# Retuning a hand-written planner: paired ramps, full P.V rounds and packs of four in a two-layer attention and gMLP kernel

## The chip, the cores and the metric

The kernel runs on one core of one Trainium2 chip. The metric is the device time in microseconds (us) of one execution; lower is better. Five executions of the kernel before took 1650.32, 1652.5, 1651.31, 1657.53 and 1656.46 us, with a median of 1652.5 us. A profile was taken of one execution, and all views below are of that one.

The engines are named as in the profile: PE (TensorE, matmuls; PEld is its weight loads), DVE (VectorE), ACT (ScalarE), POOL (GpSimd) and SP (SyncE, which issues DMAs).

## The reference

Two layers, each an attention block and a gMLP block, on one sequence of 2048 positions with width 512. The attention has 32 query heads of 16 channels that share one key and one value head.

```python
def _A_ref(x, wq, wk, wv, wo):
    q = (x @ wq).reshape(B, S, H, Dh).transpose(0, 2, 1, 3)   # H=32, Dh=16
    k = x @ wk
    v = x @ wv
    scores = einsum('bhqd,bkd->bhqk', q, k) * Dh ** (-0.5)
    o = einsum('bhqk,bkd->bhqd', softmax(scores), v)
    return o.transpose(0, 2, 1, 3).reshape(B, S, H * Dh) @ wo

def _B_ref(x, w_in, w_sp, b_sp, w_out):                        # F=1792, Fh=896
    z = gelu(x @ w_in)
    z1, z2 = z[..., :Fh], layernorm(z[..., Fh:])
    g = einsum('ts,bsf->btf', w_sp, z2) + b_sp[None, :, None]
    return (z1 * g) @ w_out

x = A_x
x = x + _A_ref(layernorm(x), ...)
x = x + _B_ref(layernorm(x), ...)
x = x + _A_ref(layernorm(x), ...)
x = x + _B_ref(layernorm(x), ...)
```

## The kernel before

The program of each engine is written out by a planner in the kernel's Python. `Sched` holds a modelled clock, a list of ready tasks for each engine and a model cost for each task; `Kernel.run` moves the modelled clock from event to event and lets each free engine take one step (`step_act`, `step_dve`, `step_pool`, `step_pe`, `step_sp`). The order in which tasks are taken becomes the fixed instruction order of that engine, with semaphore waits put in where a task needs another engine's result. So the constants at the top of `Kernel` (about L380 to L418) do not touch any instruction's work. They decide which tasks are formed, how they are grouped, and in which order each engine runs them.

**Attention.** Per layer there are 2048 score blocks. One block is 128 keys by 512 (query, head) columns, for one of four groups of PE rows j. A *pack* is one to four blocks, one per j, which PE computes side by side (`issue_pack`, matmul at L1227); each block fills one bank of PSUM, of which there are eight. `pack_ready` (L1153) says whether a pack may be issued and how large it is: up to `score_cap` banks may hold scores, 6 when the layer's first 128 blocks are out (`A.full`) and 4 before that. A pack of fewer than four is allowed only if ACT's modelled backlog is at most `ACT_LOW`.

A block's exponential is made in one of two ways:

- by ACT, as an `Exp` activation of one bank or of two adjacent banks at once (`pick_exp` L1367, `do_exp`, instruction at L1402). The result is one slot of `Pb`, a buffer of 32 slots in SBUF. Two banks at once need two adjacent banks and two adjacent free slots. With `ACT_ONE` = 3, when the queue holds one pack alone and at least three of its blocks, ACT takes a single first.
- by DVE and POOL (`dve_block` L1294), which approximate the exponential with integer arithmetic as a weighted sum of three piecewise linear *ramps*. DVE reads the scores and writes the first ramp (L1316, called an A task here). The two other ramps are made from the first one, by POOL or by DVE (`ramp_fn`, L1335, called S tasks), one slot each. `commit_ramp` (L1337) joins two S tasks of the same kind into one instruction of 1024 columns when their sources lie in adjacent slots and two adjacent slots are free.

How many blocks of a pack go the second way is a running credit in `issue_pack`: each block adds `SHARE`, `SHARE_HI` or, before a layer is full, `RAMP_SHARE`. One is held back when DVE's backlog is over `DVE_HIGH`.

**P.V.** PE multiplies each finished slot with the values, in four groups of columns j side by side (`do_pv`, L1457). Up to four matmuls, one per j, form a *round*. A block of ACT brings one matmul, a block of DVE three. `pv_depth` (L1519) says how many rounds a visit does: at most `PV_MAX`, and only if the rounds are filled to `PV_EFF`; when PE comes from another kind of work, a visit also needs `PV_LEAST` matmuls. When fewer than 8 slots are free it goes ahead anyway.

**The rest.** Queries are taken in eight chunks. When a chunk is done, its output is normalised, projected and added, and the gMLP of its rows begins (`mlp_in`: gelu on ACT in a batch, with a load of ACT's table before and after; `spatial`: the product with `w_sp`, L1083). This lies beside the attention of later chunks. After the last chunk only the last pass (`last_pass`, L1114 and L1116), the output product (L1138) and the residual (L1142) are left; each tile of 128 rows then feeds the layer norm, keys and queries of the next layer, so that layer's first blocks begin between the two. `step_pe` orders PE: gelu batches first, then a pack, then P.V, then other matmuls that fit before the next pack is due or that have waited longer than `MISC_T`.

`step_dve` takes tasks that only DVE can do first. It takes an S task only if POOL is idle and POOL's backlog is over `POOL_MAX`. `step_pool` takes whatever is ready by priority.

Of the kernel before, what the change touches and what calls it, by code (L numbers as in the profile page):

```python
# [10 lines left out]
ALU = mybir.AluOpType  # L11
# [8 lines left out]
S = 2048  # L20
# [21 lines left out]
def c_ps(cols):  # L42
    return 70 + 1.042 * cols, 130
# [49 lines left out]
class Sched:  # L93
# [69 lines left out]
    def commit(self, task, eng=None):  # L163
        t = self.t
        eng = eng or task.eng
        task.eng = eng
        if task.alts is not None:
            task.cost, task.fn = task.alts[eng]
        task.start = t
        if task.hook is not None:  # L170
            task.hook(task)
        cost = task.cost() if callable(task.cost) else task.cost
        occ, lat = cost
        if eng == "pe" and task.mode != self.pe_mode:
            occ += 100
            self.pe_mode = task.mode
        port = eng == "dve" and task.tag in PORT
        if port:
            occ += max(0.0, self.free["pool"] - t)
        end = t + occ  # L180
        self.free[eng] = end
        if port:
            self.free["pool"] = max(self.free["pool"], end)
        self.busy[eng] += occ
        task.done = end + lat
        waits = self._waits(eng, task)
        if eng == "sp":
            k = min(range(self.NDMA), key=lambda i: (self.dma_last[i].done if self.dma_last[i] else -1.0))
            prev = self.dma_last[k]
            if prev is not None:  # L190
                waits += self._wait_on(eng, prev)
            self.dma_n[k] += 16
            task.key, task.val = ("dma", k), self.dma_n[k]
            self.dma_last[k] = task
        else:
            self.cnt[eng] += 1
            task.key, task.val = eng, self.cnt[eng]
        s = dict(self.know[eng])
        if s.get(task.key, 0) < task.val:
            s[task.key] = task.val  # L200
        self.snap[(task.key, task.val)] = s
        self.prog[eng].append((waits, task.fn, task.key, task))
        self.log.append((eng, t, end, task.tag))
        if eng == "pe":
            self.pe_log.append((t, end))
        self.left -= 1
        for s_ in task.succ:
            s_.nopen -= 1
            if s_.nopen == 0:
                self._arm(s_)  # L210
        self.event(end)
        self.event(task.done)
        while self.after:
            self.after.pop(0)()
        return task
# [164 lines left out]
class Kernel:  # L380
# [1 line left out]
    SCORE_CAP = 6  # L382
    WSP_FROM = 25000
    NPS = 32
    PV_FREE = 6
    KT_ACT = 16
    CREDIT = 2
    CAP_LINE = 8000
    RAMP_SHARE = 0.3
    Q_LATE = 2  # L390
    PORT_WAIT = 0
    NWS = 8
# [1 line left out]
    GP_PRIO = 0.95  # L394
    SP_PRIO = 3.5
    NROT = (2, 2)
    SHARE = 0.3
    SHARE_HI = 0.32
    PE_LINE = 5000
    WARM = 0.6  # L400
    FILL_MIN = 2
    ACT_LOW = 1200
    POOL_MAX = 1400
    DVE_MAX = 1500
    DVE_HIGH = 2500
    PV_MIN = 3
    PV_MAX = 3
    PV_EFF = 0.7
    PV_LEAST = 4
    SLACK = 300  # L410
    SLACK_HI = 500
    MISC_T = 2000
    MISC_T2 = 1500
    MISC_T3 = 1000
    PE_LINE2 = 8000
    ACT_ONE = 3
    ACT_MAX = 2

    def __init__(self, nc, es, ins, out):
# [733 lines left out]
    def pack_ready(self):  # L1153
        if self.ai >= len(self.attns) or (self.batch is not None and not self.batch.pe_done):
            return None
        A = self.attns[self.ai]
        av = self.banks.avail()
        room = min(4, len(av), self.score_cap() - self.score_held)
        if room < self.FILL_MIN or room < 4 and self.act_backlog() > self.ACT_LOW:
            return None  # L1160
        blks = []
        deps = []
        for (u, kt, j) in A.blocks[A.nxt:A.nxt + room]:
            ds = A.kdep[kt] + [A.qdep[t] for t in range(u.q0 // P, (u.q0 + u.nq) // P)]
            if any(d.start is None or d.done > self.s.t for d in ds):
                break
            deps += ds
            blks.append((u, kt, j))
        if not blks or len(blks) < room and len(blks) < 4 and A.nxt + len(blks) < len(A.blocks) and self.act_backlog() > self.ACT_LOW:
            return None  # L1170
        return A, blks, deps, av

# [17 lines left out]
    def issue_pack(self, A, blks, deps, bs):  # L1190
        s = self.s
        k = len(blks)

        x = self.RAMP_SHARE if not A.full else self.SHARE if self.pe_line() > self.PE_LINE else self.SHARE_HI
        self.credit = min(self.credit + k * x, self.CREDIT) if x else 0.0
        late = sum(1 for u, kt, j in blks if kt >= self.KT_ACT)
        nd = min(2, k - 1, k - late, int(self.credit))
# [6 lines left out]
        aj = [i for i in range(k) if i not in dj]  # L1204

        best = None
        for act in itertools.combinations(sorted(bs, key=lambda b: b.i), len(aj)):
            runs = sum(1 for x, y in zip(act, act[1:]) if y.i != x.i + 1)
            key = (runs, sum(b.i for b in act))
            if best is None or key < best[0]:  # L1210
                best = (key, act)
        act = list(best[1])
# [38 lines left out]
        av = sum(1 for b in self.pslots.items if not b.held and b.free <= self.s.t)  # L1251
        return av - k >= sum(v for m, v in self.need.items() if m < n)

    def slot_runs(self):
        free = {b.i: b for b in self.pslots.avail()}
        runs = []
        for i in sorted(free):
            if i - 1 in free:
                runs[-1].append(free[i])
            else:  # L1260
                runs.append([free[i]])
        return sorted(runs, key=lambda r: (len(r), r[0].i))
# [5 lines left out]
    def first_slot(self):  # L1268

        runs = self.slot_runs()  # L1270
        free = {b.i: b for r in runs for b in r}
        for i in self.open_slots:
            for k in (i - 1, i + 1):
                if k in free:
                    self.open_slots.remove(i)
                    return free[k], True
        for r in runs:
            if len(r) > 1:
                return r[0], False
        return runs[0][0], False  # L1280
# [13 lines left out]
    def dve_block(self, pk, u, kt, j, bank, n):  # L1294
# [7 lines left out]
            sl[v] = b  # L1302
            self.need[n] -= 1

        def h0(task):
            b, paired = self.first_slot()
            slot(0, b, task, T)
            if not paired:
                self.open_slots.append(b.i)

            def go():
                self.free_bank(bank, task)
                u.av[j].append((task.done, task, sl[0], 1, kt))
            self.after.append(go)
        lo0 = float(TERMS[0][0])
        a = self.dve(c_ps(512), lambda e: e.tensor_scalar(self.Pi[:, sl[0].i, :], self.ps32[:, bank.i, :], EBIAS + lo0, lo0, op0=ALU.add,  # L1316
                                                          op1=ALU.max), [pk], 1.0, gate=lambda: self.slot_ok(n, 1), hook=h0, tag="A")
        for v in range(1, T):

            def hv(task, b=None, v=v):  # L1320
# [9 lines left out]
            k = self.either({"pool": (c_pool(512), fn), "dve": (c_4x(512), fn)}, [a], 3, gate=lambda: self.slot_ok(n, 1), hook=hv, tag="S")  # L1330
            k.ramp = (v, sl, n)

    def ramp_fn(self, v, src, dst, k):
        lo = float(TERMS[v][0])
        return lambda e: e.tensor_scalar(self.Pi[:, dst():dst() + k, :], self.Pi[:, src():src() + k, :], lo, 1.0, op0=ALU.add, op1=ALU.mult)  # L1335

    def commit_ramp(self, k, eng):  # L1337

        s = self.s
        v, sl, n = k.ramp  # L1340
        for it in s.arm[eng]:
            p = it[2]
            if p.ramp is None or p.start is not None or p.ready > s.t or p.ramp[0] != v or abs(p.ramp[1][0].i - sl[0].i) != 1:
                continue
            m = max(n, p.ramp[2])
            if not self.slot_ok(m, 2):
                continue
            run = self.pair_slots()
            if run is None:
                continue  # L1350
            two = sorted((k, p), key=lambda x: x.ramp[1][0].i)
            i, o = two[0].ramp[1][0].i, run[0].i
            f = Task(eng, (c_pool if eng == "pool" else c_4x)(1024), self.ramp_fn(v, lambda: i, lambda: o, 2), k.deps + p.deps, tag="S")

            def hook(task):
                for x, b in zip(two, run):
# [2 lines left out]
            s.left += 1  # L1359
            s.commit(f)  # L1360
            for x in two:
                x.start, x.done, x.key, x.val = f.start, f.done, f.key, f.val
                s.left -= 1
            return
        s.commit(k, eng)

    def pick_exp(self):  # L1367
        q = [x for x in self.act_q if x[0].done <= self.s.t][:self.ACT_MAX]
        av = sorted((b for b in self.pslots.items if not b.held and b.free <= self.s.t), key=lambda b: b.i)
        free = {b.i: b for b in av}  # L1370

        most = len(q)
# [146 lines left out]
    def pv_depth(self, pv, room):  # L1519
# [4 lines left out]
        hurry = self.pv_hurry(pv)  # L1524
        if hurry:
            most = max(most, 1)
        for r in range(most, 0, -1):
            n = sum(min(len(x), r) for x in ls)
            if hurry or n >= 4 * r * self.PV_EFF and (sw == 0 or n >= self.PV_LEAST):
                return r  # L1530
# [116 lines left out]

    def step_dve(self):
        s = self.s
        k = s.pick("dve", lambda k: k.alts is None or "pool" not in k.alts)  # L1650

        if k is None and s.free["pool"] <= s.t + self.PORT_WAIT and self.backlog("pool") > self.POOL_MAX:
            k = s.pick("dve")
# [5 lines left out]
            s.commit(k, "dve")  # L1659
        return True  # L1660

    def step_pool(self):
        k = self.s.pick("pool")
        if k is None:
            return False
        if k.ramp is not None:
# [127 lines left out]
```

## Time and profile before

| what | value |
|---|---|
| the profiled execution | 1650.3 us, span of its instructions 1648.6 us |
| median of five executions | 1652.5 us |
| score matmuls (L1227) | 4096 |
| `Exp` on two banks / on one (ACT, L1402) | 948 / 946 |
| first ramps (DVE, L1316) | 1254 |
| later ramps on POOL, two slots / one | 421 / 976 |
| later ramps on DVE, two slots / one | 236 / 218 |
| P.V matmuls (L1457) | 6604 |
| ACT busy, 50 to 762 us (layer 0) | 688 of 712 us |
| ACT busy, 762 to 890 us (between the layers) | 57 of 128 us |
| ACT busy, 890 to 1580 us (layer 1) | 664 of 690 us |

The counts give the shares: 948 x 2 + 946 = 2842 blocks on ACT and 1254 on DVE are 4096 together, and 2842 + 3 x 1254 = 6604 P.V matmuls. "Busy" of an engine is the time in which at least one of its instructions runs. A `128x512` instruction works on one slot or bank, a `128x1024` one on two.

### The profile page before, as it was taken

Reading aid. Unit: us, or ns where it says so; the run is one execution under the profiler, and the core shown is the slowest. Engines: PE = TensorE matmul, PEld = TensorE weight load, DVE = VectorE, ACT = ScalarE, POOL = GpSimd, SP = SyncE. Lnnn points to the kernel's source line nnn. Section 1 sums busy time; section 2 is a strip of 40 time slices with the busy share of each in tenths; the row PEclk is TensorE's granted clock in tenths of the full one; section 3 lists DMA queues with packets and bytes.
Section 4 is the critical chain, followed back from the end, with each engine's and each line's share of the span. In section 5 each row is a group of like instructions: output and inputs, shape, how many; then the busy total and the mean of one; then the engine's idle time right before and its main releaser. Section 6 shows DMA issues by size and latency. Waiting matters only on the chain.

```text
span 1648.6 us, 36831 instructions
## 1 busy us (share of the span) xinstructions
PE 1555.6 (94%) x14016; PEld 528.8 (32%) x14016; DVE 1404.9 (85%) x2556; ACT 1445.9 (88%) x2067; POOL 1183.0 (72%) x1616
## 2 busy tenths in 40 slices
PE   6999999999999999999998998999999999899999
PEld 3333233222322223233433332322223222322345
DVE  7799878898788887988977998798897998788877
ACT  5999999999999998995447999999998999899940
POOL 6888868778778867774456877777876778778730
PEclk8999999999999989999999999999999999999999
DMA  8000000100001110101110000011000101001021
GB/s 212 11 8 5 8 8 17 33 17 15 14 15 26 21 21 10 31 17 36 23 31 17 9 4 8 7 30 33 14 15 14 27 14 27 14 14 27 18 42 53
DMA packets 123996, 39.76 MB, mean 24 GB/s; under 512 B 116272, under 2 KB 123312, under 8 KB 123824
## 3 DMA queue, kind: packets, MB, share of 16 engines
q1 hardware_dynamic: 123824, 37.41, 10.5%
q8 instruction: 115, 1.88, 0.5%
q14 instruction: 57, 0.47, 0.1%
HBM read 6.98 MB, written 2.10 MB: 6 GB/s over the span
## 4 chain that ended last, share of the span: by engine, by line
PE 52%; ACT 31%; DVE 10%; issue 2%; POOL 2%; DMA 2%; DVEq 0%; ACTq 0%; POOLq 0%
ACT Pb L1402 30%; PE ps_all L1457 16%; PE ps_all L1227 14%; PE ps_all L1083 8%; DVE Pb L1316 4%; PE ps_all L976 3%; PE ps_all L1022 3%; PE ps_all L1138 3%; DVE Pb L1335 2%; POOL Pb L1335 2%; PE ps_all L761 1%; PE ps_all L920 1%; DMA onT<-o_norm 1%; PE ps_all L834 1%; PE ps_all L1114 1%
## 5 line engine op out<-in xcount | busy, mean ns | idle before, releaser
L1402 ACT ACTIVATE Pb<-ps_all 128x512 bf16<-128x512 f32 (+1 forms) x1894 | 1349.9, 885 | 75.4 <-PE ps_all L1227 65.2
L1335 POOL TENSOR_SCALAR Pb<-Pb 128x512 int16<-128x512 int16 (+1 forms) x1397 | 1065.1, 762 | 301.5 <-DVE Pb L1316 130.6
L1316 DVE TENSOR_SCALAR Pb<-ps_all 128x512 int16<-128x512 f32 x1254 | 830.1, 684 | 134.5 <-PE ps_all L1227 119.2
L1457 PE MATMUL ps_all<-Pb,V 128*32 128x512 bf16 x6604 | 625.6, 389 | 16.1 <-ACT Pb L1402 5.9
L1227 PE MATMUL ps_all<-Q,kT 32*128 32x512 bf16 x4096 | 570.8, 386 | 48.5 <-ACT Pb L1402 27.9
L1227 PEld LDWEIGHTS ps_all<-Q,kT 32*128 32x128 bf16 x4096 | 147.0, 91 | 540.1 <-ACT Pb L1402 307.1
L1457 PEld LDWEIGHTS ps_all<-Pb,V 128*32 128x32 bf16 x6604 | 150.3, 94 | 305.4 <-issue 123.0
L1335 DVE TENSOR_SCALAR Pb<-Pb 128x1024 int16<-128x1024 int16 (+1 forms) x454 | 205.1, 474 | 16.8 <-PE ps_all L1457 13.4
L1083 PE MATMUL ps_all<-wstr,z 128*128 128x512 bf16 x840 | 213.8, 381 | 2.7 <-POOL z L1004 0.4
L1091 DVE TENSOR_TENSOR gp<-ps_all,gp 128x512 f16<-128x512 f32 x168 | 112.9, 686 | 26.0 <-PE ps_all L1083 24.0
L1083 PEld LDWEIGHTS ps_all<-wstr,z 128*128 128x128 bf16 x840 | 67.4, 97 | 101.3 <-issue 15.5
L1138 PE MATMUL ps_all<-w_out,z 128*128 128x512 bf16 x224 | 55.9, 380 | 1.7 <-DVE z L1124 1.3
L976 PE MATMUL ps_all<-w_in,xnT 128*128 128x448 bf16 x256 | 52.4, 361 | 2.6 <-ACT Pb L1402 1.2
L1036 ACT ACTIVATE z<-ps_all 128x512 bf16<-128x512 f32 (+1 forms) x60 | 31.3, 566 | 23.6 <-PE ps_all L1022 23.6
L1022 PE MATMUL ps_all<-xnT,w_in 128*128 128x512 bf16 (+2 forms) x280 | 51.5, 337 | 0.0
L593 POOL TENSOR_SCALAR ln_rs<-ln_mv 128x1 f32<-128x1 f32 (+2 forms) x48 | 11.2, 237 | 54.7 <-DVE ln_mv L603 53.3
L818 DVE CAST oT<-ps_all 128x512 bf16<-128x512 f32 x64 | 43.7, 683 | 4.5 <-PE ps_all L1457 4.1
L989 DVE BATCH_NORM_STATS2 st<-z 128x6 f32<-128x448 bf16 x64 | 36.3, 606 | 12.4 <-ACT z L981 12.0
L1091 DVE TENSOR_TENSOR gp<-ps_all,bspc 128x512 f16<-128x512 f32 x56 | 38.5, 687 | 9.1 <-PE ps_all L1083 8.1
L602 DVE BATCH_NORM_STATS2 ln_st<-X 128x6 f32<-128x512 bf16 x64 | 43.1, 679 | 2.7 <-DMA X<-in_A_x_dram 2.5
L593 POOL TENSOR_SCALAR rs<-mv 128x4 f32<-128x4 f32 (+2 forms) x10 | 2.3, 234 | 56.0 <-DVE mv L991 56.0
L920 PE MATMUL ps_all<-wo,onT 128*128 128x512 bf16 x128 | 38.4, 387 | 3.4 <-DMA onT<-o_norm 3.4
(67 smaller groups left out, 706.4 us busy)
## 6 DMA issues: line engine op xcount, KB each, us to landing
out_dram<-X SPq DMA_DIRECT2D x16, 128.0 KB, 1.7
w_in<-in_B_w_in_dram SPq DMA_DIRECT2D x1, 1792.0 KB, 12.0
X<-in_A_x_dram SPq DMA_DIRECT2D x3, 512.0 KB, 6.5
bspc<-in_B_b_sp_dram SPq DMA_DIRECT2D x8, 128.0 KB, 3.5
w_out<-in_B_w_out_dram SPq DMA_DIRECT2D x1, 896.0 KB, 12.7
wstr<-in_B_w_sp_dram SPq DMA_TRANSPOSE x40, 3.9
X<-in_A_x_dram SPq DMA_DIRECT2D x2, 256.0 KB, 3.0
wq<-in_A_wq_dram SPq DMA_DIRECT2D x1, 512.0 KB, 4.6
```

The costliest lines, as they stand in the source:

```text
L818: ev = Task("dve", c_ps(512), lambda e, u=u, k=k: e.tensor_copy(self.oT[:, k, :], self.ps32[:, u.bank.i, :]), [self.oT_use[k]], 0.2, tag=" ...
L920: ins = e.matmul(self.ps32[:, b, :], self.onT[:, c, t % 4, :], self.wo[:, c, :], start=(c == 0), stop=(c == 3))
L976: ins = e.matmul(self.ps32[:, b, 0:448], self.xnT2[:, buf, kd, o:o + P], self.w_in[:, kd, FH + h * 448:FH + (h + 1) * 448], start=(kd == 0 ...
L1022: ins = e.matmul(self.ps32[:, b, i * nq:(i + 1) * nq], self.w_in[:, kd, f * P:(f + 1) * P], self.xnT2[:, buf, kd, 0:nq], start=(kd == 0), ...
L1083: ins = e.matmul(self.ps32[:, b, :], self.z2[:, (s0 + i) % 8, f * P:(f + 1) * P], self.wstr[:, sl[i // 4][1] + i % 4, :], start=(i == 0), ...
L1091: return Task("dve", c_ps(512), lambda e: e.tensor_tensor(self.gp[:, tc, f, :], self.ps32[:, bank(), :], src, ALU.add), dps, 1.05, tag="gp")
L1138: ins = e.matmul(self.ps32[:, b, :], self.z1[:, tc, f, o:o + P], self.w_out[:, f, :], start=(f == 0), stop=(f == NF - 1))
L1227: ins = e.matmul(self.ps32[:, jb[i].i, :], self.kT[32 * j:32 * j + 32, u.half, kt * P:(kt + 1) * P], q, tile_position=(32 * j, 0), start=T ...
L1316: a = self.dve(c_ps(512), lambda e: e.tensor_scalar(self.Pi[:, sl[0].i, :], self.ps32[:, bank.i, :], EBIAS + lo0, lo0, op0=ALU.add, op1=AL ...
L1335: return lambda e: e.tensor_scalar(self.Pi[:, dst():dst() + k, :], self.Pi[:, src():src() + k, :], lo, 1.0, op0=ALU.add, op1=ALU.mult)
L1402: return e.activation(self.Pb[:, s0:s0 + n, :], self.ps32[:, b0:b0 + n, :], ACTF.Exp, scale=ESCALE)
L1457: ins = e.matmul(self.ps32[32 * j:32 * j + 32, u.bank.i, :], self.V[:, var, kt, :], self.Pb[:, sl.i, :], tile_position=(0, 32 * j), start= ...
```

## The change

The change edits constants and decision rules of the planner. No kind of instruction is new; what is computed stays the same, apart from which blocks are approximated by ramps.

- Shares: `SHARE`/`SHARE_HI` 0.30/0.32 become 0.32/0.34. `RAMP_SHARE` becomes 0.32 for layer 0 and 0 for layer 1 (`RAMP_SHARE1`).
- Before layer 1 is full, only packs of four are issued (`FILL_R`, `ACT_LOW_R`).
- `ACT_LOW` 1200 becomes 1400, `DVE_HIGH` 2500 becomes 1800, `ACT_ONE` 3 becomes 9.
- P.V: at most two rounds a visit, filled to 0.97, and six matmuls at least after other work.
- Slots next to a lone first ramp are kept free of exponentials while at least 8 others are free (`kept`), and banks are chosen so that DVE's blocks come to lie side by side (`A_ADJ`).
- DVE looks first for a pair of later ramps when POOL is idle and has over 4000 ns of backlog; POOL starts nothing when it has such a backlog and DVE will be free within 200 ns.
- Other matmuls count as late earlier (`MISC_T` 2000/1500/1000 become 1000/1000/500), and the planner's cost of a change of PE mode is 110 in place of 100.

`A_TWO`, `PAIRS` and `PV_R` are 0, so what they guard does not run.

```diff
@@ Kernel
-    PV_FREE = 6
+    PV_FREE = 8
+    A_TWO = 0
+    KEEP = 8
+    PAIRS = 0
+    POOL_TOP = 4000
+    HOLD = 200
+    A_ADJ = 1
-    RAMP_SHARE = 0.3
+    RAMP_SHARE = 0.32
-    SHARE = 0.3
-    SHARE_HI = 0.32
+    SHARE = 0.32
+    SHARE_HI = 0.34
+    FILL_R = 4
+    ACT_LOW_R = 0
+    PV_R = 0
+    RAMP_SHARE1 = 0.0
-    ACT_LOW = 1200
+    ACT_LOW = 1400
-    DVE_HIGH = 2500
+    DVE_HIGH = 1800
-    PV_MAX = 3
-    PV_EFF = 0.7
-    PV_LEAST = 4
+    PV_MAX = 2
+    PV_EFF = 0.97
+    PV_LEAST = 6
-    ACT_ONE = 3
+    ACT_ONE = 9
@@ pack_ready
-        if room < self.FILL_MIN or room < 4 and self.act_backlog() > self.ACT_LOW:
+        low = self.ACT_LOW if A.full or A.layer == 0 else self.ACT_LOW_R
+        if room < (self.FILL_MIN if A.full or A.layer == 0 else self.FILL_R) or room < 4 and self.act_backlog() > low:
             return None
@@ issue_pack
-        x = self.RAMP_SHARE if not A.full else self.SHARE if self.pe_line() > self.PE_LINE else self.SHARE_HI
+        x = (self.RAMP_SHARE, self.RAMP_SHARE1)[A.layer] if not A.full else self.SHARE if self.pe_line() > self.PE_LINE else self.SHARE_HI
...
+        pend = [it[2].ramp[3] for it in s.arm["dve"] if it[2].tag == "A" and it[2].start is None]
         for act in itertools.combinations(sorted(bs, key=lambda b: b.i), len(aj)):
             runs = sum(1 for x, y in zip(act, act[1:]) if y.i != x.i + 1)
-            key = (runs, sum(b.i for b in act))
+            rest = sorted([b.i for b in bs if b not in act][:nd] + pend)
+            key = (runs - self.A_ADJ * sum(1 for x, y in zip(rest, rest[1:]) if y == x + 1), sum(b.i for b in act))
@@ slots: kept() is new; slot_runs() and pick_exp() leave its slots out
+    def kept(self):
+        if not self.KEEP:
+            return set()
+        free = {b.i for b in self.pslots.avail()}
+        r = set()
+        for i in self.open_slots:
+            for k in (i + 1, i - 1):
+                if k in free and k not in r:
+                    r.add(k)
+                    break
+        return r if len(free) - len(r) >= self.KEEP else set()
@@ step_dve
-        k = s.pick("dve", lambda k: k.alts is None or "pool" not in k.alts)
+        k = None
+        if s.free["pool"] <= s.t + self.PORT_WAIT and self.backlog("pool") > self.POOL_TOP:
+            k = self.ramp_pair("dve")
+        if k is None:
+            k = s.pick("dve", lambda k: k.alts is None or "pool" not in k.alts)
@@ ramp_pair() is new: a ready later ramp whose neighbour is ready too
+    def ramp_pair(self, eng):
+        s = self.s
+        rs = [it[2] for it in s.arm[eng] if it[2].ramp is not None and it[2].ramp[0] and it[2].start is None and it[2].ready <= s.t]
+        at = {(k.ramp[0], self.place(k)): k for k in rs}
+        if len(rs) < 2 or self.pair_slots() is None:
+            return None
+        for k in rs:
+            p = at.get((k.ramp[0], self.place(k) + 1))
+            if p is not None and self.slot_ok(max(k.ramp[2], p.ramp[2]), 2):
+                s.arm[eng] = [i for i in s.arm[eng] if i[2] is not k]
+                return k
+        return None
@@ step_pool
+        if s.t < s.free["dve"] <= s.t + self.HOLD and self.backlog("pool") > self.POOL_TOP:
+            return False
```

## The prediction, written before the result

> **What bounds the kernel now.** I read the page first (busy time and the 40 slices), then busy time by stage, then ACT's waits in one stage, then the groups kept apart by shape, and last a stretch of PE's order.
>
> Page, busy time, and ACT's row of the slices:
>
> ```profile
> PE 1555.6 (94%) x14016; PEld 528.8 (32%) x14016; DVE 1404.9 (85%) x2556; ACT 1445.9 (88%) x2067; POOL 1183.0 (72%) x1616
> ...
> ACT  5999999999999998995447999999998999899940
> ```
>
> The averages put PE first. The slices say otherwise: ACT is full but for the start, four slices in the middle and the end. Busy time of the stages (us; PE, PEld, DVE, ACT, POOL):
>
> ```profile
> 50.00:762.00 712.00, 681.80 (x6148) 213.90 (x6147) 612.78 (x1094) 688.06 (x986) 552.02 (x729) 0.99 0.08 16
> 762.00:890.00 128.00, 117.85 (x1048) 53.84 (x1045) 107.68 (x221) 57.03 (x84) 58.45 (x104) 0.99 0.16 33
> 890.00:1580.00 690.00, 655.47 (x5959) 207.82 (x5957) 594.01 (x1051) 664.45 (x950) 536.95 (x704) 1.00 0.08 17
> ```
>
> Waits of ACT from 50 to 762 us (us in total, times, longest):
>
> ```profile
> ACT z L1036 <- PE ps_all L1022: 10.9, 16, 1.1
> ACT Pb L1402 <- PE ps_all L1227: 5.9, 17, 1.0
> ACT z L981 <- PE ps_all L976: 3.0, 8, 0.8
> ACT Pb L1402 <- PE ps_all L1457: 2.1, 5, 1.0
> ```
>
> In layer 0 ACT idles 24 of 712 us, and 14 of these are gelu batches. Its exponentials wait 9 us. So ACT's work sets the pace of the two long stretches. Between them ACT has half its time free, and PE (118 of 128) and DVE (108) take turns on the chain.
>
> Groups by shape (busy us, mean ns of one, idle before):
>
> ```profile
> L1402 ACT ACTIVATE Pb<-ps_all 128x1024 bf16<-128x1024 f32 x948 | 952.9, 1098 | 47.6 <-PE ps_all L1227 42.8 <-PE ps_all L1457 2.6 <-DVE Pb L1335 0.6
> L1402 ACT ACTIVATE Pb<-ps_all 128x512 bf16<-128x512 f32 x946 | 546.3, 671 | 27.8 <-PE ps_all L1227 22.4 <-PE ps_all L1457 3.5 <-DVE Pb L1335 0.5
> L1335 POOL TENSOR_SCALAR Pb<-Pb 128x512 int16<-128x512 int16 x976 | 616.0, 631 | 224.4 <-DVE Pb L1316 108.2 <-PE ps_all L1457 44.5 <-PE ps_all L1227 8.4
> L1335 DVE TENSOR_SCALAR Pb<-Pb 128x1024 int16<-128x1024 int16 x236 | 131.7, 573 | 7.8 <-PE ps_all L1457 5.0 <-POOL Pb L1335 0.4
> ```
>
> The means are latencies, and neighbours overlap. The distance from one start to the next is the price; its medians in the trace are 904 ns for a double `Exp`, 478 for a single, 608 for a first ramp, 700 and 1127 for a single and a double ramp on POOL. PE's order, 163 to 166 us (start, us):
>
> ```profile
> 163.36 0.39 PE L1227 MATMUL ps_all<-Q,kT 32*128 32x512 bf16 x3
> 163.69 0.40 PE L1457 MATMUL ps_all<-Pb,V 128*32 128x512 bf16 x4
> 164.02 0.39 PE L1227 MATMUL ps_all<-Q,kT 32*128 32x512 bf16 x2
> 164.34 0.62 PE L761 MATMUL ps_all<-z,wq 128*128 128x128 bf16 x8
> ```
>
> A pack and a round of P.V each cost about 0.32 us however many of the four lanes are filled.
>
> **What the Trainium skill says.** "TensorEngine Tiling (Array Packing)", Key Properties: a change of tiling mode drains PE. The trace agrees: a lone round goes from start to start in 332 ns, two rounds in 547, so 215 for a round and about 115 for the change. "SBUF — State Buffer", Who interferes with whom: a VectorE instruction in a two-port mode and a GpSimd instruction exclude each other for a whole instruction, and the later one waits. The trace agrees: of DVE's 236 double ramps, 139 began while POOL was running and took 681 ns on average; the other 97 took 419. "Perfetto Trace Analysis", Identifying the Most-Contended Engine: matmul busy time is no measure of PE's headroom. Here PE is 96% busy in a stretch where ACT hardly waits for it.
>
> **The change, part by part.**
>
> *Shares.* Of 4096 blocks, 256 come before a layer is full and 3840 after. Before: about 0.30 x 256 = 77 of the 1254 first ramps fall in the 256, so 1177 in the 3840. The constants rise by 0.02: 77 more blocks go to DVE in ACT's full stretches. At about 460 ns a block on ACT that is at most 36 us. `DVE_HIGH` at 1800 holds some back, and held credit is lost above 2; as far as it cuts deeper than now it could cost half as much (+18). DVE must find 77 x 0.6 = 46 us, of 99 idle in layer 0 and 96 in layer 1; the 154 further ramps cost about 0.5 us each on POOL, 77 of some 310 idle. They fit, but DVE and POOL are needed in time, not on average. I take 60%: **-21 us** (-36 to +18).
>
> *Pairs on ACT.* Without the single-first rule a pack of three gives a double first, and the third may join the next pack. Two singles cost 956, a double 904: 52 ns a pair. There are 886 singles in the two stretches (454 and 432), so all of them would give 23 us. Packs stay small (I count 1530 packs, 2.7 blocks on average), and one block is often alone after DVE's share. I take a quarter: 111 pairs, **-6 us** (-23 to 0). Slots kept for ramps narrow the choice of two adjacent ones; that is why not more.
>
> *Ramps on DVE and POOL.* A double on DVE that finds POOL idle saves 262 ns over one that waits; over 139 it is 36 us of DVE. POOL's hold costs at most 0.2 us each time. No chain runs through it while ACT is full; this is what makes room for the 46 us above. Counted at **0**; if DVE were the bound it would be worth up to those 36 us.
>
> *P.V in full rounds.* I count 1260 visits with 5.2 matmuls on average, about 1900 rounds where 6604/4 = 1651 are needed. After: 6604 + 2 x 39 = 6682 matmuls (39 more ramp blocks net: 77 more when full, 38 fewer before), 835 visits of two rounds at 0.548 us, 458 us against 581 now. PE gains some 120 us, but ACT hides it: ACT waits 9 us for PE in layer 0. The price is in slots: finished slots wait until every lane has two. POOL waited 65 us on P.V for slots already, ACT 6. I take **+4** (0 to +80).
>
> *Between the layers.* The 128 first blocks of layer 1 lose 0.3 x 128 = 38 first ramps. That frees DVE of 38 x 0.6 = 23 us and PE of 76 P.V matmuls. From 800 to 890 us the trace has 132 blocks in 55 packs and 208 P.V matmuls in 44 visits; after, 33 packs (22 x 0.32 = 7 us off PE) and about 130 matmuls in 17 visits of 0.55 (some 9 us against 20). The last pass, keys and layer norm gain from both: of 90 us, perhaps 20. Against it: with a cap of four banks, a pack of four waits until all four banks are free. PE 0.32, two doubles 1.8, and about 0.2 until PE sees it make 2.3 us a pack, 74 us for 32, near the 90 there are. The blocks wait for keys as well, tile by tile. I take **-8** (-20 to +15).
>
> *The other constants.* Lateness of other matmuls and the cost of 110 only reorder PE, which has room: 0. `ACT_LOW` at 1400 makes small packs come sooner; PE pays 0.32 each out of the 120 us: 0. The start and the 69 us of PE after the last `Exp` stay.
>
> Sum: -21 - 6 + 4 - 8 = -31. From the profiled execution's 1650.3 this gives 1619.3; the median of the runs stands 2.2 higher, so I say **1621**.
>
> **The rivals.**
> - *Everything lands (12%).* ACT's work falls by 36 and 23 us, its waits for PE in both stretches (18) go with PE's new room, and 20 come between the layers: -97, of which contention leaves about 75: **1577**. For it: PE gains 120 us. Against: 52 ns a pair needs neighbours in banks and slots at once.
> - *DVE and POOL become the bound (20%).* ACT gives up work that they do not finish in time; first ramps already have DVE waiting on packs (56 us in layer 0), and POOL on first ramps (56). Then only pairs and the middle remain, about -10: **1642**, ranging over no change.
> - *Slower: slots run out (20%).* P.V waits for full rounds, `Pb` fills, and ACT stands before a P.V visit. At 835 visits, each 10 ns that ACT waits costs 8 us; from 37 ns a visit the 31 us are gone. At 60 ns: +50 - 31 = **1671**. For it: 32 slots, some kept free. Against: ACT waited only 6 us on P.V, and below 8 free slots P.V goes anyway.
>
> **How the numbers follow.** The forecast has 48%. Its own range is 1605 to 1638. Of the second rival about a fifth lies within 0.3% (5 us, what can be told apart here) and a tenth is slower. Faster: 48 + 12 + 14 = 74%; same 4%; slower 2 + 20 = 22%. The range for 8 in 10 leaves out the far half of the first rival and of the third: 1590 to 1668.
>
> **What would show it.** Right: about 1295 first ramps, none for layer 1 before it is full; ACT full with some 2800 blocks; P.V visits near 8; double ramps on DVE near 420 ns; the middle below 128 us. Wrong: ACT idle in the long stretches behind P.V or packs, fewer first ramps than 1254, more singles, or a longer middle.

## The result, and the profile after

The changed kernel takes 1649.8 us (median of 29 executions, 1640.5 to 1655.5). The kernel before takes 1653.6 us in 50 executions shared with it. The ratio is 0.9968 with a 95% interval of 0.9958 to 0.9977: 3.8 us faster at the medians, where 31 were forecast. The profiled execution took 1651.3 us with a span of 1649.6, so it lies 1.5 us above its median. The profiled one before lay 3.2 below the median of the 50, which is why the two spans (1648.6 and 1649.6) do not show the gain.

The page of the changed kernel, busy time, the slices of DVE, ACT and the clock granted to PE, and the chain that ended last:

```profile
PE 1516.2 (92%) x14216; PEld 506.9 (31%) x14216; DVE 1452.7 (88%) x2624; ACT 1442.9 (87%) x2052; POOL 1111.2 (67%) x1378
...
DVE  7899989999799898998865999799897999799887
ACT  5999989999899898996479989899998999899950
...
PEclk7899899999999899999999999999899999999999
...
PE 45%; DVE 28%; ACT 23%; issue 3%; DMA 1%; POOL 0%; SPq 0%; DVEq 0%; POOLq 0%
```

The same line of the kernel before:

```profile
PE 52%; ACT 31%; DVE 10%; issue 2%; POOL 2%; DMA 2%; DVEq 0%; ACTq 0%; POOLq 0%
```

DVE's part of the chain has gone from 10% to 28%, and ACT's from 31% to 23%. ACT makes fewer exponentials now (2802 blocks, 2842 before). ACT's row has eights where it had nines, and the clock has more dents.

By stage (busy us of PE, PEld, DVE, ACT and POOL), to be read beside the same rows in the prediction:

```profile
50.00:762.00 712.00, 663.42 (x6222) 204.54 (x6223) 645.79 (x1138) 671.68 (x977) 535.09 (x637) 0.98 0.08 17
762.00:890.00 128.00, 113.84 (x1162) 55.04 (x1166) 88.90 (x192) 84.93 (x109) 26.23 (x54) 1.00 0.15 29
890.00:1580.00 690.00, 636.96 (x5984) 194.73 (x5976) 626.70 (x1100) 648.20 (x917) 517.11 (x612) 0.98 0.10 16
```

In the first stretch ACT now idles 40 us (24 before), and DVE is busy 646 us (613 before). In the same stretch the score matmuls of PE wait longer for banks that DVE's first ramps still hold (us in total, times, longest; the kernel before, then the changed one):

```profile
PE ps_all L1227 <- DVE Pb L1316: 3.8, 9, 0.8
PE ps_all L1240 <- DVE Pb L1362: 15.0, 40, 1.0
```

The stages can be timed by the score matmuls, counted in order of their starts:

| stage (us) | before | after | difference |
|---|---|---|---|
| start to block 128 of layer 0 | 67.2 | 69.7 | +2.5 |
| block 128 to the last block of layer 0 | 693.8 | 700.1 | +6.3 |
| last block of layer 0 to block 128 of layer 1 | 124.5 | 112.3 | -12.2 |
| block 128 of layer 1 to the end | 763.1 | 767.5 | +4.4 |

So the middle brought what was forecast and more, and the two long stretches, which were to bring most of the 31 us, did not get faster. Together they are 10.7 us longer here; some 5 us of that is only the distance of these two executions from their medians. The groups of the changed kernel by shape (busy us, mean ns of one, idle before) show where:

```profile
L1367 DVE TENSOR_SCALAR Pb<-Pb 128x1024 int16<-128x1024 int16 x371 | 220.8, 615 | 7.4 <-PE ps_all L1503 6.0
L1367 DVE TENSOR_SCALAR Pb<-Pb 128x512 int16<-128x512 int16 x111 | 41.1, 376 | 3.3 <-PE ps_all L1503 3.3
L1367 POOL TENSOR_SCALAR Pb<-Pb 128x1024 int16<-128x1024 int16 x576 | 617.8, 1073 | 153.8 <-DVE Pb L1362 79.1 <-PE ps_all L1503 31.1 <-DVE Pb L1367 8.9
L1448 ACT ACTIVATE Pb<-ps_all 128x1024 bf16<-128x1024 f32 x923 | 921.3, 1067 | 53.8 <-PE ps_all L1240 41.5 <-PE ps_all L1503 5.4 <-DVE Pb L1367 1.2
```

DVE has 371 double ramps (236 before), but one takes 615 ns (573 before). Of the 371, 204 began while POOL was running (with at least 30 ns of its instruction left) and took 776 ns on average; the other 167 took 417. These are called collisions below. In 144 of the 204 the double ended 270 to 290 ns after the POOL instruction that it had met: it waited for POOL to end. A double takes 418 ns and a single 284 with POOL idle. What DVE's ramps take beyond that is called their *excess* here: 83 us in all, against 55 before.

One such place, DVE and then POOL from 700 us on in the timeline (start us, length us):

```profile
700.69 1.88 DVE L1362 TENSOR_SCALAR Pb<-ps_all 128x512 int16<-128x512 f32 x3
702.49 1.18 DVE L1367 TENSOR_SCALAR Pb<-Pb 128x1024 int16<-128x1024 int16 x1
703.59 0.67 DVE L1101 TENSOR_TENSOR gp<-ps_all,gp 128x512 f16<-128x512 f32 x1
```

```profile
700.09 4.05 POOL L1367 TENSOR_SCALAR Pb<-Pb 128x1024 int16<-128x1024 int16 x4 [0.51 <-PE ps_all L1503]
```

POOL runs four ramps end to end, and the double on DVE takes 1.18 us in the middle of them. In the plan POOL stands aside here: the planner keeps it free until the double is done. But the plan only orders each engine's own instructions; waits are written for results that a task needs, and POOL's next ramp needs nothing of DVE's double. Its inputs are there, so it starts.

### The profile page after: what moved, and what is told of

Its sections match the earlier page's. It is cut to its first block, busy times and chain, and to the rows that moved or that the text cites. A ratio compares the mean times of both kernels' runs of the same rounds, so it can differ in the third digit from the quotient of the medians.

```text
span 1649.6 us, 36882 instructions
## 1 busy us (share of the span) xinstructions
PE 1516.2 (92%) x14216; PEld 506.9 (31%) x14216; DVE 1452.7 (88%) x2624; ACT 1442.9 (87%) x2052; POOL 1111.2 (67%) x1378
## 4 chain that ended last, share of the span: by engine, by line
PE 45%; DVE 28%; ACT 23%; issue 3%; DMA 1%; POOL 0%; SPq 0%; DVEq 0%; POOLq 0%
ACT Pb L1448 22%; DVE Pb L1362 14%; PE ps_all L1503 12%; PE ps_all L1240 12%; DVE Pb L1367 8%; PE ps_all L1093 7%; PE ps_all L986 3%; PE ps_all L1032 3%; PE ps_all L1148 3%; DVE gp L1101 2%; PE ps_all L771 1%; DVE ln_st L612 1%; DVE oT L828 1%; DVE X L934 1%; PE ps_all L930 1%
## 5 line engine op out<-in xcount | busy, mean ns | idle before, releaser
L1367 POOL TENSOR_SCALAR Pb<-Pb 128x512 int16<-128x512 int16 (+1 forms) x1159 | 990.5, 855 | 340.1 <-DVE Pb L1362 194.5
L1362 DVE TENSOR_SCALAR Pb<-ps_all 128x512 int16<-128x512 f32 x1294 | 843.2, 680 | 90.7 <-PE ps_all L1240 81.2
L1240 PE MATMUL ps_all<-Q,kT 32*128 32x512 bf16 x4096 | 587.4, 392 | 89.9 <-ACT Pb L1448 33.3
L1503 PE MATMUL ps_all<-Pb,V 128*32 128x512 bf16 x6684 | 533.4, 394 | 15.4 <-DVE Pb L1367 4.4
L1240 PEld LDWEIGHTS ps_all<-Q,kT 32*128 32x128 bf16 x4096 | 152.7, 91 | 621.6 <-ACT Pb L1448 364.2
L1367 DVE TENSOR_SCALAR Pb<-Pb 128x1024 int16<-128x1024 int16 (+1 forms) x482 | 258.8, 560 | 10.8 <-PE ps_all L1503 9.4
L1503 PEld LDWEIGHTS ps_all<-Pb,V 128*32 128x32 bf16 x6684 | 120.0, 95 | 239.6 <-issue 119.0
L771 PE MATMUL ps_all<-z,wq 128*128 128x128 bf16 x512 | 41.1, 225 | 2.0 <-DVE Pb L1362 1.7
```

The costliest lines, as they stand in the source:

```text
L1240: ins = e.matmul(self.ps32[:, jb[i].i, :], self.kT[32 * j:32 * j + 32, u.half, kt * P:(kt + 1) * P], q, tile_position=(32 * j, 0), start=T ...
L1503: ins = e.matmul(self.ps32[32 * j:32 * j + 32, u.bank.i, :], self.V[:, var, kt, :], self.Pb[:, sl.i, :], tile_position=(0, 32 * j), start= ...
```

## The experiments

Sixteen kernels ran. Times are medians, and each ratio is to the kernel before in runs shared with it. For those that keep the plan of the changed kernel, every engine has the same instructions in the same order, but for what the edit names. The expectations say *port* for what a double of DVE and an instruction of POOL exclude each other from, as the prediction describes it. *Half clock* is time in which the profile shows PE at half its clock.

**Does POOL's missing wait cost the gain, or does the clock?** Theory 1: the collision just shown. Theory 2: PE runs at half clock more often, 51 us of the profiled execution, 17 before (counted in stretches that begin between 60 and 1600 us).

*e1_hold*: each POOL instruction also waits for the two-port instruction of DVE that the plan put before it.

```diff
         port = eng == "dve" and task.tag in PORT
+        if eng == "pool" and self.last_port is not None:
+            task.extra.append(self.last_port)
+        if port:
+            self.last_port = task
```

> The changed kernel with the same plan, and one thing more in the emitted programs: each GpSimd instruction waits for the VectorE ramp, layer-norm or z2 instruction in a two-port mode that the plan put before it. Theory 1 (the room that GpSimd leaves exists in the plan only; nothing in the program makes GpSimd wait, so it starts its next ramp and VectorE's double ramp stands behind it): double ramps on VectorE that begin while GpSimd runs fall from 204 of 371 to under 80, their mean from 615 to under 500 ns, and the time falls by 8 to 15 us below the 1649.8 of the changed kernel. Theory 2 (TensorE's clock drops to half more often, 51 us of the stretches in place of 17): the time stays within 3 us. Rival to both: GpSimd waits for VectorE too long and its ramps come late: 3 to 15 us slower.

Measured 1606.3 us, ratio 0.9708 (0.9683 to 0.9733). Its groups and its chain:

```profile
L1372 DVE TENSOR_SCALAR Pb<-Pb 128x1024 int16<-128x1024 int16 x371 | 154.1, 435 | 6.9 <-PE ps_all L1508 5.0
L1372 DVE TENSOR_SCALAR Pb<-Pb 128x512 int16<-128x512 int16 x111 | 35.4, 325 | 4.3 <-PE ps_all L1508 4.2
```

```profile
ACT 47%; PE 41%; DVE 7%; issue 3%; DMA 2%; POOL 1%; DVEq 0%; SPq 0%; ACTq 0%
```

The same place as above, with the wait (DVE, then POOL):

```profile
680.11 1.87 DVE L1367 TENSOR_SCALAR Pb<-ps_all 128x512 int16<-128x512 f32 x3
681.90 0.41 DVE L1372 TENSOR_SCALAR Pb<-Pb 128x1024 int16<-128x1024 int16 x1
```

```profile
679.67 2.17 POOL L1372 TENSOR_SCALAR Pb<-Pb 128x1024 int16<-128x1024 int16 x2 [0.55 <-PE ps_all L1508]
682.40 1.04 POOL L1372 TENSOR_SCALAR Pb<-Pb 128x1024 int16<-128x1024 int16 x1 [0.56 <-DVE Pb L1372]
```

POOL pauses 0.56 us, and the double takes 0.41 in place of 1.18. Over the whole run 97 doubles instead of 204 begin under a running POOL, and DVE's ramps take 11 us too long in place of 83. ACT has the chain again. The gain of 43 us is about three times the 15 us that were expected at most, though fewer collisions went than expected (97 left, not under 80). Theory 1 holds, and the size of its effect was far underrated. Half clock fell as well, to 14 us, so this run alone does not rule theory 2 out.

*e2_fill* and *e3_both*: 150 rounds with zero weights in the gaps that the plan leaves on PE, without and with the wait.

```diff
+            gap = y[3].start - (x[3].done - 225)
+            k = int((gap - (0 if "pv" in (x[3].mode, y[3].mode) else 220)) // 216)
...
+            out += [([], fn, None, None)] * max(k, 0)
```

> The changed kernel with the same plan, and 150 rounds of matmuls with zero weights put into gaps of 216 ns or more that the plan leaves on TensorE. They add nothing to the output. Theory 2 (half clock): stretches at half clock after 60 us fall from 51 us to under 15, and the time falls by 8 to 15 us. Theory 1 (port): the clock improves, but the time stays within 3 us or rises by 1 to 5, since the fillers take TensorE's time in front of packs.

> Both edits together, plan unchanged. If both theories hold, their gains add: 16 to 30 us below 1649.8. If only one holds, it equals that one alone.

e2_fill took 1645.3 us (0.9941, 0.9919 to 0.9963) with 7 us at half clock, DVE's excess unchanged at 84 us. e3_both took 1601.8 (0.9683, 0.9657 to 0.9709) with 3 us. Both are 4.5 us below their partner without fillers; for e2_fill that lies between what the two theories said. The intervals overlap, so a gain of the clock is not clearly shown; what it can be worth is some 5 us and not the 43.

*e4_before_hold*: the wait of e1 in the kernel before.

> The kernel before with the same wait of GpSimd behind VectorE's two-port instructions, plan unchanged. Theory 1 says that this matters where VectorE is late and ScalarE waits through TensorE; in the kernel before ScalarE is full, so within 4 us of before, though 139 double ramps that began under a running GpSimd become fewer. If it gains 8 us or more, the port was a bound before as well.

1643.6 us, 0.993 (0.9905 to 0.9955), some 10 to 12 us, which is over the 4 expected: the collisions cost the kernel before as well, with DVE's excess down from 55 to 22 us. With the wait in both kernels, the change is worth 37 us (1643.6 to 1606.3).

**Is it the port, or keeping the engines in step?** *e5_early* was meant as a control: POOL waits for the instruction just before the double.

```diff
         if port:
-            self.last_port = task
+            self.last_port = self.last_dve
+        if eng == "dve":
+            self.last_dve = task
```

> A control for the held wait: the changed kernel with the same plan, and GpSimd waits as often, but for the VectorE instruction that comes just before the two-port one, so that it may still start ahead of the double ramp. Port theory: double ramps that begin under a running GpSimd stay near 200 of 371, and the time stays within 5 us of the changed kernel's 1649.8. Rival (the gain of the held wait, 1606.3, came from keeping the two engines in step and not from the port): it gains 20 us or more as well.

It took 1603.2 us (0.9682, 0.9654 to 0.9709), so the expectation failed. Its trace says why it was no control: only 60 doubles began under a running POOL, and DVE's excess was 7 us. POOL could now start at the earliest when DVE was free for its double, DVE came first, and POOL stood behind it: POOL's ramps took 28 us longer than in e1_hold. The collision had changed sides, and POOL has time. The chain is that of e1_hold, not of the changed kernel:

```profile
ACT 47%; PE 38%; DVE 9%; issue 3%; DMA 1%; POOL 1%; SPq 0%; DVEq 0%; ACTq 0%
```

*e11_step2* waits for the instruction two places before, so that POOL may start first again.

> The changed kernel with the same plan, and GpSimd waits for the VectorE instruction two places before a two-port one. That binds GpSimd to VectorE's order in 95 of its 1374 instructions more than the changed kernel does, where the wait one place before does in 293, and it lets GpSimd start a ramp before the double. Port theory: the time follows the ns that VectorE's ramps take over 418 and 284: if collisions stay above 60 us in total, the time stays within 10 us of 1649.8; if they fall to half, it comes half the way to 1603. Rival (step, not port): the gain is 25 us or more though the collisions stay.

1647.8 us (0.9961, 0.9944 to 0.9978), the same as the changed kernel; 190 collisions, excess 85 us. The mean of its doubles and the shares of DVE and ACT in its chain are as in the changed kernel:

```profile
L1375 DVE TENSOR_SCALAR Pb<-Pb 128x1024 int16<-128x1024 int16 x371 | 221.2, 616 | 6.8 <-PE ps_all L1511 5.5
...
PE 43%; DVE 28%; ACT 23%; issue 4%; DMA 1%; POOL 1%; SPq 0%; DVEq 0%; ACTq 0%; POOLq 0%
```

A wait that leaves the collisions brings nothing that can be told. It binds in fewer places than e5's (95 against 293), so a share of "step" in e5 is not excluded, but it is not needed.

*e16_hold_layer0*: the wait of e1, up to 780 us of the plan.

> The changed kernel with the held wait in the first layer only (until 780 us of the plan). If the gain sits where the collisions are: the 700 us of layer 0's scores (block 128 to the last) fall to about 680 as with the wait everywhere, those after block 128 of layer 1 stay near 767, and the time is 1626 to 1632. If one place made the whole gain, it is near 1606 or near 1650.

1624.0 us (0.9815, 0.9788 to 0.9841). Block 128 to the last block of layer 0 takes 677 us (700 without, 680 with the wait everywhere), and block 128 of layer 1 to the end 763 (767 without, 743 with). The gain lies where the wait is. Over the eight kernels with this one plan (e12_early_fill below among them) the time follows the excess: with 83 to 85 us of it they take 1645 to 1650 us, with 49 (this one) 1624, and with 7 to 11 they take 1601 to 1606.

**What each part of the change is worth, with the wait and without.** These kernels set constants back and are planned anew, so their whole order differs.

```diff
 e8, e13    SHARE 0.30  SHARE_HI 0.32  RAMP_SHARE 0.3  DVE_HIGH 2500
 e9, e14    FILL_R 2  ACT_LOW_R 1200  RAMP_SHARE1 0.3
 e10, e15   PV_FREE 6  PV_MAX 3  PV_EFF 0.7  PV_LEAST 4
 e6, e7     POOL_TOP out of reach: no ramp pair first on DVE, no room left by POOL
```

> The changed kernel without the rule that VectorE takes a pair of later ramps first and GpSimd leaves room for it (its threshold set out of reach), all other constants as changed. The plan gives VectorE 300 doubles in place of 371 and GpSimd more. Port theory: fewer doubles meet a running GpSimd (under 150), but GpSimd has more ramps, so the ramps are late on the other side: 1650 to 1665 us. Rival (the rule itself costs what the rest of the change gains): it is faster than the changed kernel by 10 us or more.

> The same without that rule, with the held wait of GpSimd behind VectorE's two-port instructions. Port theory: the wait recovers less than the 43 us that it recovers with the rule, since there are fewer collisions to take away: 1630 to 1650. If it comes to 1610 or below, the rule adds nothing once the port is kept free.

> The changed kernel with the held wait, and the shares of ramps and the limit of VectorE's backlog as before (about 1221 first ramps in place of 1294). With the port kept free ScalarE sets the pace again, so the blocks given to VectorE count: 8 to 20 us slower than the 1606.3 with the changed shares. Rival (VectorE is the bound even so): not slower, or faster.

> The changed kernel with the held wait, and the rules between the layers as before (ramps allowed, packs of two and three allowed in layer 1 before it is full). The stretch from the last score matmul of layer 0 to block 128 of layer 1 was 124.5 us before and 112.3 after the change. Theory: it goes back to 120 to 125, and the time is 8 to 15 us above the 1606.3 with the held wait. Rival (the shorter middle is paid back in layer 1): within 5 us.

> The changed kernel with the held wait, and the rules for P.V as before (three rounds a visit, filled to 0.7, four matmuls at least). The plan needs about 200 visits and 100 us of TensorE more. If full rounds are hidden behind ScalarE, as predicted: within 5 us of 1606.3. If TensorE's room is what lets packs come in time: 15 to 30 us slower, and ScalarE waits more for score matmuls. Half clock should fall below the 13.7 us in either case.

> The changed kernel with shares and VectorE's limit as before, without any added wait. Port theory: VectorE, held up by collisions, is the bound in the changed kernel, so giving it fewer blocks costs nothing: within 6 us of 1649.8, or faster. Rival (ScalarE is the bound, as predicted): 10 to 25 us slower, as with the held wait (22 us).

> The changed kernel with the rules between the layers as before, without any added wait. The middle goes from 112.3 us to between 115 and 125; if it is a stage by itself, 6 to 14 us slower than 1649.8.

> The changed kernel with the rules for P.V as before, without any added wait. Clock theory: TensorE is busier, half clock falls from 51 us to under 15, which is worth 4 to 5 us by the fillers; against it about 200 visits more. Port theory: VectorE is the bound, so P.V's form matters little: within 8 us of 1649.8. With the held wait it cost 17 us.

| set back | without the wait: us, ratio | with the wait: us, ratio |
|---|---|---|
| nothing | 1649.8, 0.9968 (0.9958 to 0.9977) | 1606.3, 0.9708 (0.9683 to 0.9733) |
| shares | 1640.7, 0.9921 (0.9894 to 0.9948) | 1628.3, 0.9821 (0.9793 to 0.9849) |
| middle | 1653.1, 0.9983 (0.9967 to 0.9998) | 1620.6, 0.9808 (0.9783 to 0.9833) |
| P.V | 1653.9, 0.9998 (0.9983 to 1.0014) | 1622.9, 0.9828 (0.9806 to 0.9849) |
| pair first | 1659.3, 1.0016 (0.9999 to 1.0033) | 1644.0, 0.9931 (0.9905 to 0.9956) |

The row of the shares is the key (it sets the limit of DVE's backlog back as well). As changed, the kernel is *faster* with the old shares, by 8 us by the ratios; with the wait it is 19 to 22 us slower with them. Handing blocks from ACT to DVE pays only if DVE can do its ramps in the time that the plan gives them. Here are DVE's doubles and first ramps in e13_share:

```profile
L1362 DVE TENSOR_SCALAR Pb<-ps_all 128x512 int16<-128x512 f32 x1221 | 804.9, 682 | 121.1 <-PE ps_all L1240 110.3 <-PE ps_all L1503 2.0
L1367 DVE TENSOR_SCALAR Pb<-Pb 128x1024 int16<-128x1024 int16 x319 | 176.8, 568 | 8.5 <-PE ps_all L1503 4.0
```

There are 73 first ramps fewer than after the change, the excess is 62 us in place of 83, and ACT has 47% of the chain (23% in the changed kernel). All other rows of the table cost more to undo with the wait (14 us or more) than without (2 to 10; for the middle the intervals overlap, so nothing is shown there): this fits that DVE's lateness covered most of what the parts bring. The losses do not add up: undone one at a time with the wait they come to some 90 us, and the whole change is worth 37. The largest is the pair rule. Without it the kernel with the wait takes 1644.0 us, as long as the kernel before with the wait (1643.6). Not all of that is the rule's own, since e7 also has more excess (23 us, 11 in e1_hold) and more half clock (44 us, 14). Not all expectations were met. In e6 175 doubles collided, where under 150 were expected. In e9 the middle took 114.7 us, not 120, so most of its loss lies later: block 128 of layer 1 to the end takes 753 us, 743 with the changed rules. In e14 the middle took 118, as expected, but the time rose by only 3 us and not by 6 to 14. In e10 ACT did not wait more for score matmuls, though that was expected of a run as slow as this. In e15 half clock fell to 3 us and the time did not fall, though with more P.V work on PE.

*e12_early_fill* joins the wait of e5 with the fillers.

> The wait one place before together with the 150 filler rounds. The fillers took 4.5 us off the changed kernel and off the one with the held wait, so 1603.2 less 3 to 5: 1598 to 1600. If the wait alone has already removed the half clock (6.8 us were left), no gain.

1601.0 us (0.9687, 0.9668 to 0.9707), not to be told from e5_early or e3_both. Versions with either wait beat both kernels, by about 3%.

## Why the prediction was wrong

- **What bounds the kernel.** Right in the main for the kernel before, though its own collisions cost 10 to 12 us there (e4). The step from there, that ACT would still set the pace after the change, failed in the changed kernel: ACT's idle time in layer 0 rose from 24 to 40 us, and PE's score packs waited 15 us for banks that DVE frees (4 before, 1.5 in e1_hold). With the wait it is right, with ACT at 47% of the chain.
- **Ramps on DVE and POOL, counted at 0.** This is the step that failed. I wrote that a double that finds POOL idle saves 262 ns, and that this "makes room" for the 46 us of new first ramps, and I took the plan's room for real. I had the count of 139 collisions in front of me, in a plan that already took DVE's ramps only when POOL was idle, and I did not ask what makes POOL wait in the program. Nothing does. More doubles met a running POOL (204), at 359 ns each in place of 262, and DVE lost 29 us more than before. How much that is worth shows in e1_hold, where taking 72 us of the excess away brought 43. Nor was the rule worth nothing: with the wait, undoing it costs 37 us, near the 36 that I had named for the case that DVE is the bound. That the two sizes agree may be chance, since the 36 came from the collisions before.
- **Shares, -21.** The count was right (1294 first ramps, 1295 forecast). Together with the limit of DVE's backlog the worth was +8 to +9 without the wait and -19 to -22 with it. I had bounded it at +18 on the bad side for another reason, the limit of DVE's backlog.
- **Pairs on ACT, -6.** Nothing came: 923 doubles and 956 singles, against 948 and 946. Two thirds of ACT's blocks were in doubles before and after.
- **P.V in full rounds, +4 and hidden.** The rounds became fuller: of 1012 visits counted in the trace (835 forecast) 677 have eight matmuls. By the count that gave 581 us before, the visits take 507, so PE gained 74 us and not 120. Slots did not run out; ACT's wait for P.V rose from 6 to 10 us in all. But it was not hidden: undoing it costs 4 to 5 us without the wait, and 17 to 20 with it. In e10 the middle takes 119 us instead of 112.4, and the stretch from block 128 of layer 1 to the end 12 us more. PE's part of the chain is larger in e10 than in e1_hold, 50% and 41%. Which wait carries that was not found; ACT's wait for score matmuls hardly differs (42 and 47 us). So the full rounds gained time where I had forecast a cost: I had taken PE's room as worthless while ACT is full.
- **Between the layers, -8.** The middle became shorter by more than that, 12.2 us, but not by these rules alone: setting them back lengthens it by 6 us (e14) or 2 (e9), and setting P.V back by 7 (e15 and e10). That no first ramps fall there and that packs are whole did not starve ACT, which is busy 85 us there instead of 57.
- **The other constants and PE's room, 0.** PE's room had a price that I left out: half clock for 51 us instead of 17. By the fillers it is at most some 5 us.
- **The rivals.** The second one, DVE and POOL becoming the bound, is what happened, though I put it down to work not finished in time and not to collisions. The one in which slots run out did not occur. With the wait the kernel lands below the forecast, at 1606.3 against 1621, and with the wait in both kernels the change is worth 37 us, near the 31 of the sum. That is luck, for the terms differ: the pairs on ACT brought nothing, P.V gained where a cost was forecast, and the pair rule on DVE, counted at 0, is the largest.

## What to carry to other kernels

An order planned across engines holds on the chip only where a semaphore enforces it. If a plan keeps two engines off a shared resource, write that down as a wait, and check in the trace that an instruction which is to find the resource free takes its short time. Before pricing work handed from one engine to another, price what the receiving engine loses to collisions now; a mean well above the shortest time of the same shape is the sign.

## What the hardware showed that was not expected

- In 50 places a double on DVE took over 1.1 us where the same double took under 0.43 in e1_hold. In all 50 POOL's own ramp had started at most 0.24 us ahead, and the double ended 277 to 281 ns after that ramp did: DVE waited for the whole length of it. "SBUF — State Buffer", Who interferes with whom, in the Trainium skill says that issue order decides who blocks; the trace agrees, and e5_early turned it round.
- With the new rules for P.V, PE runs at half clock more often: 51 us in the changed kernel and 3 with the old rules (e15), 14 and 0 with the wait (e1, e10). In the changed kernel, each of the nine stretches at half clock after 60 us follows a window of 3.4 us in which, counting 0.42 ns for each column of a matmul (215 ns for a round of 512 columns, by the prediction), PE streamed 34 to 47% of the time; the median of all windows is 73%. "TensorE: Matmul & The Clock Gate", What's actually happening, in the Trainium skill gives the window as about 3.4 us, which agrees with the stretches of 3.4, 6.8 and 10.2 us here. So here a drop follows windows that are a third to nearly half full, with no pause over 1.6 us in them. That the low share is the cause was not tried by itself, though the fillers of e2_fill cut half clock from 51 to 7 us. It is not the whole rule: on the same grid of windows, four with 44 to 46% are not followed by a drop.
